# Six products in place of ten for M, with normalized queries regrouped into blocks of 120 features

## The chip, the cores and the metric

One core of one Trainium2 chip. The metric is the device time of one execution in microseconds (us), taken as the median of several runs. Engines are named as the profile names them: PE (TensorE matmul), PEld (its weight loads), DVE (VectorE), ACT (ScalarE), POOL (GpSimd) and SP, whose queue issues most of the DMAs.

## The reference

Two branches are computed from the same x and mixed by a gate. The part that matters here is the linear attention:

```python
B, S, D = 1, 2048, 640;  H = 32;  Dh = 20
pq, pk = phi(q), phi(k)                       # q, k, v = x @ wqkv
kv  = einsum("bhsd,bhse->bhde", pk, v)
num = einsum("bhqd,bhde->bhqe", pq, kv)
den = einsum("bhqd,bhd->bhq", pq, sum_s pk)
a   = (num / den) @ wo
out = g * a + (1 - g) * mlp_branch(x)         # layernorm, w1, shift, w2, layernorm, w3 (F=1728), w4
```

The kernel turns `num @ wo` around: M = blockdiag(kv) @ wo is one 640 x 640 matrix, and a = (pq / den) @ M. The branch with w1 to w4 (called W1 to W4 below) is far more work and shares TensorE with it.

## The kernel before

Every engine has a fixed instruction list. The order of work in it is made while the kernel is built, by a list scheduler that models the engines; each item is placed when its predecessors are done in the model. So any change can reorder the whole list.

M is built from kv, which has blocks of 20 x 20 on the diagonal. Six groups of heads (six heads of 20 features each: 120 rows; the last group has two heads: 40 rows) are multiplied with their rows of wo. M is stored in five tiles of 128 rows, and 120 does not divide 128, so most tiles get rows from two groups: ten products of 640 columns in all. In the code `Lt` holds the masked blocks of kv and `wo_aug` the rows of wo.

```python
PAIRS = []                                   # the ten (group r, tile j) overlaps
for r in range(6):
    f0, f1 = 120 * r, min(120 * r + 120, D)
    j0, j1 = f0 // 128, (f1 - 1) // 128
    for j in range(j0, j1 + 1):
        a0, a1 = max(f0, 128 * j), min(f1, 128 * (j + 1))
        PAIRS.append((r, j, a0, a1))

def m_group(j):
    prs = [(pi, r) for pi, (r, jj, a0, a1) in enumerate(PAIRS) if jj == j]
    b1, b2 = bank(), bank()
    mm_group(ps[:, b1, 0:512], [(Lt[0:nrow(r), pi, :], wo_aug[0:nrow(r), r, 0:512]) for pi, r in prs])
    mm_group(ps[:, b2, 0:128], [(Lt[0:nrow(r), pi, :], wo_aug[0:nrow(r), r, 512:D]) for pi, r in prs])
    activation(M_sb[:, j, 0:512], ps[:, b1, 0:512], ACTF.Copy)
    copy(dve, M_sb[:, j, 512:D], ps[:, b2, 0:128])
# ... cut ...
def qn_scale(t):                             # pq / den, in place, on DVE
    # ... cut: dnr[:, 1, sd, :] = 1 / den
    dve(lambda e: e.tensor_tensor(pq3, pq3, dnr[:, 1, sd, :].unsqueeze(2).to_broadcast([128, H, DH]), ALU.mult), ...)
def qt_tile(t):                              # DMA transpose to pqnT, on the SP queue
    sch.dma("sp", pqnT[:, :, 128 * t:128 * (t + 1)], pq_tok[:, t, :], ..., transpose=True)
def a_tile(t):                               # a = pqn @ M
    # ... cut ...
    mm_group(ps[:, b, 0:512], [(pqnT[:, j, tok], M_sb[:, j, 0:512]) for j in range(KD)])
    mm_group(ps[:, b + 1, 0:128], [(pqnT[:, j, tok], M_sb[:, j, 512:D]) for j in range(KD)])
```

After the last W2 tile, DVE adds its result to x_tok, ACT forms the sum of squares (`junk<-x_tok`), POOL computes the statistics of four tiles (`st`) and normalizes them one by one (`xn<-x_tok,st`), and the SP queue transposes each (`xnT<-xn`). The pqnT transposes stand behind the last of these in the same queue, and the first product with M_sb needs the first pqnT transpose.

## Time and profile before

| | before |
|---|---|
| median of the first 3 runs | 265.46 us (265.42 to 265.71) |
| span of the profiled run | 264.6 us |
| PE busy | 258.2 us, 98% |
| M's ten products on PE | 129.84 to 135.13 us |
| first product with M_sb | 139.58 us |

The profile's page of the kernel before, busy time and instruction counts by engine:

```profile
span 264.6 us, 4264 instructions
## 1 busy us (share of the span) xinstructions
PE 258.2 (98%) x1675; PEld 136.4 (52%) x1707; DVE 145.9 (55%) x242; ACT 107.6 (41%) x216; POOL 91.1 (34%) x148
```

PE is the bound.

PE's timeline of the kernel before, in the stage of M (start us, us until the last end, then line, operation, tiles, shape and count):

```profile
129.84 0.71 PE L606 MATMUL ps<-wo_aug,Lt 120*128 120x512 bf16 x4
130.38 1.24 PE L606 MATMUL ps<-xnT,w_58 128*128 128x512 bf16 x5
131.46 1.25 PE L606 MATMUL ps<-wo_aug,Lt 120*128 120x512 bf16 x8
132.77 1.02 PE L606 MATMUL ps<-xnT,w_58 128*128 128x512 bf16 x4
133.63 1.56 PE L606 MATMUL ps<-wo_aug,Lt 120*128 120x512 bf16 x8
135.13 0.62 PE L1025 MATMUL ps<-xnT,w_58 128*64 128x512 bf16 x4
```

The ten products (each a 512-column and a 128-column matmul) stand in three bursts between W3 groups of five matmuls.

The chain of waits of the kernel before, around the second burst:

```profile
131.66 0.60 ACT h2T L662
132.26 0.50 ACT M_sb L662
132.76 0.01 issue
132.77 2.43 PE ps L606 x12
```

It says that PE waited for ACT to empty a bank at 132.77.

Two lines from POOL's and DVE's timelines of the kernel before become important later, when the first normalization of the last four tiles runs. POOL:

```profile
129.18 0.88 POOL L628 TENSOR_SCALAR xn<-x_tok,st_55 128x640 bf16<-128x640 bf16 x1
```

DVE at that time (the last bracket is idle time ahead of an instruction and what ended it):

```profile
128.42 0.82 DVE L1035 TENSOR_REDUCE dnr<-qprod 128x32 f32<-128x640 f32 x1
130.58 0.29 DVE L671 CAST M_sb<-ps 128x128 bf16<-128x128 f32 x1 [1.35 <-PE ps L606]
```

The normalization took 0.88 us, while DVE stood still for 1.35 us waiting for M's products.

### The profile page before, as it was taken

Reading aid. Unit: us, or ns where it says so; the run is one execution under the profiler, and the core shown is the slowest. Engines: PE = TensorE matmul, PEld = TensorE weight load, DVE = VectorE, ACT = ScalarE, POOL = GpSimd, SP = SyncE. Lnnn points to the kernel's source line nnn. Section 1 sums busy time; section 2 is a strip of 40 time slices with the busy share of each in tenths; the row PEclk is TensorE's granted clock in tenths of the full one; section 3 lists DMA queues with packets and bytes.
Section 4 is the critical chain, followed back from the end, with each engine's and each line's share of the span. In section 5 each row is a group of like instructions: output and inputs, shape, how many; then the busy total and the mean of one; then the engine's idle time right before and its main releaser. Section 6 shows DMA issues by size and latency. Waiting matters only on the chain.

```text
span 264.6 us, 4264 instructions
## 1 busy us (share of the span) xinstructions
PE 258.2 (98%) x1675; PEld 136.4 (52%) x1707; DVE 145.9 (55%) x242; ACT 107.6 (41%) x216; POOL 91.1 (34%) x148
## 2 busy tenths in 40 slices
PE   7999999999999999999999999999999999999996
PEld 3655555555555454554444545554545455545553
DVE  0397877899903797999786886312212121122242
ACT  3486767742365758675661031212211222121000
POOL 4003996849774017487821104001110011021020
DMA  6775898551666895253666731120000200002011
GB/s 203 244 103 147 205 146 149 162 115 24 102 121 104 299 373 82 54 99 60 69 124 124 110 68 25 33 93 0 2 0 0 102 0 0 2 0 99 2 50 50
DMA packets 50595, 24.77 MB, mean 94 GB/s; under 512 B 41996, under 2 KB 49165, under 8 KB 50576
## 3 DMA queue, kind: packets, MB, share of 16 engines
q1 hardware_dynamic: 49328, 21.23, 36.3%
q0 software_dynamic: 1152, 3.28, 5.4%
q8 instruction: 13, 0.21, 0.3%
q14 instruction: 6, 0.05, 0.1%
q10 hardware_dynamic: 96, 0.00, 0.0%
HBM read 12.05 MB, written 2.62 MB: 55 GB/s over the span
## 4 chain that ended last, share of the span: by engine, by line
PE 96%; DMA 1%; issue 1%; ACT 0%; DVE 0%
PE ps L606 60%; PE ps L1103 21%; PE ps L786 8%; PE ps L858 2%; DMA x_tok<-in_A_x_dram 1%; PE ps L1085 1%; PE ps L1025 1%; PE ps L617 1%; PE ps L859 1%; PE ps L944 1%; DVE x_tok L645 0%; PE ps L834 0%; ACT h2T L662 0%; ACT M_sb L662 0%
## 5 line engine op out<-in xcount | busy, mean ns | idle before, releaser
L662 ACT ACTIVATE h2T<-ps 128x512 bf16<-128x512 f32 x52 | 31.0, 597 | 86.5 <-PE ps L606 86.5
L606 PE MATMUL ps<-xnT,w_58 128*128 128x512 bf16 x250 | 59.0, 379 | 0.5
L1103 PE MATMUL ps<-w_84,h2T 128*128 128x128 bf16 (+1 forms) x412 | 58.2, 298 | 0.4 <-issue 0.3
L628 POOL TENSOR_SCALAR abx<-x_tok,stg 128x640 f32<-128x640 bf16 x16 | 13.9, 874 | 107.6 <-DVE x_tok L645 71.0
L1103 PEld LDWEIGHTS ps<-w_84,h2T 128*128 128x128 bf16 x416 | 32.4, 98 | 27.8 <-issue 2.1
L645 DVE SCALAR_TENSOR_TENSOR x_tok<-ps,stg,abx 128x640 bf16<-128x640 f32 (+2 forms) x17 | 14.3, 844 | 50.7 <-PE ps L1103 50.7
L606 PEld LDWEIGHTS ps<-xnT,w_58 128*128 128x128 bf16 x260 | 24.3, 98 | 24.9 <-issue 0.4
L645 DVE SCALAR_TENSOR_TENSOR abx<-ps,stg,abx 128x640 f32<-128x640 f32 x16 | 14.1, 882 | 28.5 <-PE ps L606 25.5
L662 ACT ACTIVATE Er<-ps 128x640 bf16<-128x640 f32 x32 | 22.4, 704 | 12.7 <-PE ps L606 8.5
L662 ACT ACTIVATE hsT<-ps 128x512 bf16<-128x512 f32 (+1 forms) x32 | 18.9, 593 | 14.6 <-PE ps L606 14.3
L661 ACT ACTIVATE junk<-x_tok 128x640 bf16<-128x640 bf16 x32 | 23.6, 736 | 2.0 <-DVE x_tok L643 1.7
L606 PE MATMUL ps<-M_sb,pqnT 128*128 128x128 bf16 (+1 forms) x157 | 23.7, 298 | 0.2
L606 PE MATMUL ps<-w_60,hsT 128*128 128x128 bf16 (+1 forms) x158 | 23.6, 298 | 0.1
L786 PE MATMUL ps<-pk_tok,x_tok 128*128 128x128 bf16 (+1 forms) x156 | 23.3, 297 | 0.2
L606 PE MATMUL ps<-xnT,w_59 128*128 128x512 bf16 x96 | 23.2, 379 | 0.3 <-issue 0.2
L606 PE MATMUL ps<-wkg,xT 128*128 128x131 bf16 (+1 forms) x148 | 22.4, 298 | 0.1
L606 PEld LDWEIGHTS ps<-M_sb,pqnT 128*128 128x128 bf16 x160 | 13.3, 98 | 12.4 <-issue 0.4
L606 PEld LDWEIGHTS ps<-w_60,hsT 128*128 128x128 bf16 x160 | 13.3, 98 | 12.2
L628 POOL TENSOR_SCALAR xn<-x_tok,st_54 128x640 bf16<-128x640 bf16 x16 | 17.4, 1090 | 4.7 <-DMA xnT<-xn 4.6
L606 PE MATMUL ps<-wq,xT 128*128 128x128 bf16 (+1 forms) x118 | 18.2, 298 | 0.1
L628 POOL TENSOR_SCALAR xn<-x_tok,st_55 128x640 bf16<-128x640 bf16 x16 | 16.3, 1028 | 3.6 <-DMA xnT<-xn 3.2
L628 DVE TENSOR_SCALAR Er<-Er 128x640 bf16<-128x640 bf16 x32 | 12.0, 375 | 9.4 <-ACT Er L662 9.2
(74 smaller groups left out, 264.2 us busy)
## 6 DMA issues: line engine op xcount, KB each, us to landing
w_58<-in_B_w_dram SPq DMA_DIRECT2D x1, 2160.0 KB, 8.2
w_84<-in_B_w_dram SPq DMA_DIRECT2D x1, 2080.0 KB, 13.6
x_tok<-in_A_x_dram SPq DMA_DIRECT2D x3, 640.0 KB, 5.5
out_dram<-x_tok SPq DMA_DIRECT2D x3, 640.0 KB, 3.3
wq<-in_A_wqkv_dram SPq DMA_DIRECT2D x5, 160.0 KB, 4.4
wkg<-in_A_wqkv_dram SPq DMA_DIRECT2D x5, 160.0 KB, 4.4
wv<-in_A_wqkv_dram POOLq DMA_DIRECT2D x1, 800.0 KB, 6.3
wo_aug<-in_A_wo_dram POOLq DMA_DIRECT2D x5, 150.0 KB, 5.1
```

The lines of the kernel that those rows point to most:

```text
L606: ins = e.matmul(out_ap, l, r, start=(i == 0), stop=(i == n - 1))
L617: ins = e.transpose(o, s_, ident[:])
L628: return engf(lambda e: e.tensor_scalar(out_ap, in_ap, s1, s2, op0, op1), rd, [out_ap], cost=cost)
L645: return dve(lambda e: e.scalar_tensor_tensor(out_ap, in0, scalar, in1, op0, op1), rd, [out_ap], cost=cost)
L661: return act(lambda e: e.activation(out_ap, in_ap, func, bias=bias, scale=scale, accum_out=accum), rd, wr, cost=cost)
L662: return act(lambda e: e.activation(out_ap, in_ap, func, bias=bias, scale=scale), rd, wr, cost=cost)
L786: ins = e.matmul(o, l, r, start=(t0 + q_ == 0), stop=(t0 + q_ == NT - 1))
L858: e.matmul(ps[:, b, 0:512], l, w[:, k, 0:512], start=(k == 0), stop=(k == KD - 1))
L859: return e.matmul(ps[:, b + 1, 0:n2], l, w[:, k, 512:512 + n2], start=(k == 0), stop=(k == KD - 1))
L944: ins = e.matmul(o, l, r_, start=st_, stop=sp_, skip_group_check=True)
L1025: ins = e.matmul(o, l, r, start=st, stop=sp)
L1103: ins = e.matmul(o, l, r, start=False, stop=(i == KFF - 1))
```

## The change

The features of the normalized queries are regrouped: each block of 128 columns of pq / den now holds the 120 features of one head group, plus 8 of the 40 features of the last two heads. Then a tile of M takes its first 120 rows from one group, and six products are enough. The last two heads' product gives 40 rows, which five small DMAs place in rows 120 to 127 of the five tiles. The scaling multiply writes the new layout and is split in two (600 and 40 elements). To leave its source intact it writes one slot lower, so `pq_tok` has a slot more. M is emptied by ACT alone, and its products are spread out, one after every second W3 group of the first chunk.

```diff
-    pq_tok = pa.alloc("pq_tok", [128, NT, D], BF16)
-    Lt = pa.alloc("Lt", [128, 10, 128], BF16)
+    pq_tok = pa.alloc("pq_tok", [128, NT + 1, D], BF16)
+    Lt = pa.alloc("Lt", [128, 6, 128], BF16)
+    Mt = pa.alloc("Mt", [128, D], BF16)
 ... (the queries are written to slot t + 1; the mask products follow the new layout, six in place of ten)
-    def m_group(j):
-        prs = [...]
-        ... (two banks, products of all pairs of tile j, ACT copies 512 columns, DVE 128)
+    def m_group(r):
+        n = min(R6, D - R6 * r)
+        b = pair()
+        mm_group(ps[:, b, 0:512], [(Lt[0:n, r, :], wo_aug[0:n, r, 0:512])])
+        mm_group(ps[:, b + 1, 0:128], [(Lt[0:n, r, :], wo_aug[0:n, r, 512:D])])
+        src = psf[0:n, 512 * b:512 * b + D]
+        dst = M_sb[0:n, r, :] if r < 5 else Mt[0:n, :]
+        activation(dst, src, ACTF.Copy)
+
+    def m_tail():
+        for j in range(KD):
+            sch.dma("sp", M_sb[R6:128, j, :], Mt[8 * j:8 * j + 8, :], "mt", group_total=KD)
 ...
-    for j in range(KD):
-        IT.add("KVF", ("m", j), 0.57, ..., deps=[(("lt", 0), 2.6), (("lt", 1), 1.0)] if j == 0 else [])
+    for n, r in enumerate((5, 0, 1, 2, 3, 4)):
+        IT.add("KVF", ("m", r), 0.0, ..., deps=[(("lt", 1), 1.0), (("w3", 0, 1 + 2 * n), 0.0)])
+    IT.add("MT", ("mt",), 0.0, m_tail, deps=[(("m", 5), 1.5), (("t1", NT - 1), 0.0)])
 ...
-        dve(... tensor_tensor(pq3, pq3, 1/den broadcast, ALU.mult) ...)          # 640 elements
+        for o, i0, i1, cost in (main, tail):                                     # 600 and 40 elements
+            dve(lambda e, o=o, i0=i0, i1=i1: e.tensor_tensor(o, i0, i1, ALU.mult), ...)
```

More of the change, by code (lines that the diff above doesn't have):

```diff
@@ L842, in q_tile @@
         mm_group(ps[:, b + 1, 0:128], [(xT[:, k, tok], wq[:, k, 512:D]) for k in range(KD)])
-        phi(b, pq_tok[:, t, :])
+        phi(b, pq_tok[:, t + 1, :])
     def stream(order, w, n2, done):
@@ L867, in q_four @@
                  (2, 1), (1, 4), (2, 2), (2, 3), (2, 4), (3, 1), (3, 2), (3, 3), (3, 4)]
-        stream(order, wq, 128, lambda t, b: phi(b, pq_tok[:, t, :]))
+        stream(order, wq, 128, lambda t, b: phi(b, pq_tok[:, t + 1, :]))
     def k_out(t, b):
@@ L917, in _build @@
         IT.add("GT", ("g", i), 1.36, lambda i=i: gt_step(i, NT - 5, NT), deps=[(("g0", NT - 1), 0.0)])
-    PAIRS = []
-    for r in range(6):
-        f0, f1 = 120 * r, min(120 * r + 120, D)
-        j0, j1 = f0 // 128, (f1 - 1) // 128
-        for j in range(j0, j1 + 1):
-            a0, a1 = max(f0, 128 * j), min(f1, 128 * (j + 1))
-            PAIRS.append((r, j, a0, a1))
     kv_bank = {}
@@ L949, in lt_evac @@
         b = kv_bank[h]
-        for pi, (r, j, a0, a1) in enumerate(PAIRS):
-            if (r >= 4) != (h == 1):
-                continue
-            q_ = r - 4 * h
+        for q_, r in enumerate(range(4) if h == 0 else range(4, 6)):
             n = min(R6, D - R6 * r)
-            src = ps[0:n, b, R6 * q_ + a0 - R6 * r:R6 * q_ + a1 - R6 * r]
-            msk = mask[0:n, :, :].rearrange("p b d -> p (b d)")[:, a0 - R6 * r:a1 - R6 * r]
-            tt(dve, Lt[0:n, pi, a0 - 128 * j:a1 - 128 * j], src, msk, ALU.mult)
-        bank_hold.difference_update((b, b + 1))
-    def nrow(r):
-        return min(R6, D - R6 * r)
-    def m_group(j):
-        prs = [(pi, r) for pi, (r, jj, a0, a1) in enumerate(PAIRS) if jj == j]
-        b1, b2 = bank(), bank()
-        mm_group(ps[:, b1, 0:512], [(Lt[0:nrow(r), pi, :], wo_aug[0:nrow(r), r, 0:512]) for pi, r in prs])
-        mm_group(ps[:, b2, 0:128], [(Lt[0:nrow(r), pi, :], wo_aug[0:nrow(r), r, 512:D]) for pi, r in prs])
-        activation(M_sb[:, j, 0:512], ps[:, b1, 0:512], ACTF.Copy)
-        copy(dve, M_sb[:, j, 512:D], ps[:, b2, 0:128])
+            src = ps[0:n, b, R6 * q_:R6 * q_ + n].rearrange("p (h m i) -> p h m i", m=5, i=4)
+            msk = mask[0:n, 0:n // DH, :].rearrange("p h (m i) -> p h m i", i=4)
+            if r < 5:
+                dst = Lt[0:n, r, 0:n].rearrange("p (h m i) -> p h m i", m=5, i=4)
+            else:
+                dst = Lt[0:n, r, 0:n].rearrange("p (m h i) -> p h m i", m=5, i=4)
+            tt(dve, dst, src, msk, ALU.mult)
+        bank_hold.difference_update((b, b + 1))
+    def m_group(r):
[9 more added lines that the diff above has]
+            sch.dma("sp", M_sb[R6:128, j, :], Mt[8 * j:8 * j + 8, :], "mt", group_total=KD)
     def zb_group():
@@ L979, in _build @@
         IT.add("KVF", ("lt", h), 0.0, lambda h=h: lt_evac(h), deps=[(("kvt", h), 0.0)])
-    for j in range(KD):
-        IT.add("KVF", ("m", j), 0.57, lambda j=j: m_group(j), deps=[(("lt", 0), 2.6), (("lt", 1), 1.0)] if j == 0 else [])
+    for n, r in enumerate((5, 0, 1, 2, 3, 4)):
+        IT.add("KVF", ("m", r), 0.0, lambda r=r: m_group(r), deps=[(("lt", 1), 1.0), (("w3", 0, 1 + 2 * n), 0.0)])
+    IT.add("MT", ("mt",), 0.0, m_tail, deps=[(("m", 5), 1.5), (("t1", NT - 1), 0.0)])
     IT.add("ZB", ("zb",), 0.0, zb_group, deps=[(("z", NT - 1), 1.7), (("w2", 0), 0.0)])
@@ L1033, in qn_sum @@
         sd = slot("dnr", 4)
-        tt(dve, qprod[:, :], pq_tok[:, t, :], zb[:, :], ALU.mult)
+        tt(dve, qprod[:, :], pq_tok[:, t + 1, :], zb[:, :], ALU.mult)
         dve(lambda e: e.tensor_reduce(dnr[:, 0, sd, :], qprod[:, :].rearrange("p (h d) -> p h d", d=DH),
@@ L1041, in qn_scale @@
         sd = qn_slot[t]
-        pq3 = pq_tok[:, t, :].rearrange("p (h d) -> p h d", d=DH)
         ts(dve, dnr[:, 0, sd, :], dnr[:, 0, sd, :], EPS_PHI, None, ALU.add, ALU.bypass)
         dve(lambda e: e.reciprocal(dnr[:, 1, sd, :], dnr[:, 0, sd, :]), [dnr[:, 0, sd, :]], [dnr[:, 1, sd, :]], cost=350.0)
-        dve(lambda e: e.tensor_tensor(pq3, pq3, dnr[:, 1, sd, :].unsqueeze(2).to_broadcast([128, H, DH]), ALU.mult),
-            [pq3, dnr[:, 1, sd, :]], [pq3], cost=900.0)
+        blk = pq_tok[:, t, :].rearrange("p (j c) -> p j c", c=128)
+        main = (blk[:, :, 0:R6].rearrange("p j (a d) -> p j a d", d=DH),
+                pq_tok[:, t + 1, 0:5 * R6].rearrange("p (j a d) -> p j a d", a=6, d=DH),
+                dnr[:, 1, sd, 0:30].rearrange("p (j a) -> p j a", a=6).unsqueeze(3).to_broadcast([128, 5, 6, DH]), 850.0)
+        tail = (blk[:, :, R6:128].rearrange("p m (h i) -> p h m i", i=4),
+                pq_tok[:, t + 1, 5 * R6:D].rearrange("p (h m i) -> p h m i", h=2, i=4),
+                dnr[:, 1, sd, 30:32].unsqueeze(2).unsqueeze(3).to_broadcast([128, 2, 5, 4]), 150.0)
+        for o, i0, i1, cost in (main, tail):
+            dve(lambda e, o=o, i0=i0, i1=i1: e.tensor_tensor(o, i0, i1, ALU.mult),
+                [i0, dnr[:, 1, sd, :]], [o], cost=cost)
     def qt_tile(t):
@@ L1188, in _build @@
         c = t // 4
-        deps = [(("qt", t), 3.0), (("w4load",), 0.0), (("m", KD - 1), 1.0)]
+        deps = [(("qt", t), 3.0), (("w4load",), 0.0), (("m", KD - 1), 1.0), (("mt",), 2.5)]
         if t >= 4:
```

## The prediction

> **What bounds the kernel.** TensorE (PE): the page's busy table gives PE 258.2 of 264.6 us (98%), VectorE (DVE) 145.9, ScalarE (ACT) 107.6; the chain that ended last is 96% PE; the clock was 1.00 throughout (windows view). Start-to-start distances in the trace: a 512-column matmul every 216 ns, a 128-column one every 55 ns, with 128 or 120 rows alike. So one 640-column product costs 0.271 us of PE. This agrees with the Trainium skill, "TensorE: Matmul & The Clock Gate", section "Step-by-step: what each phase is for": streaming costs N cycles, the row count does not matter.
>
> **What M costs now.** Ten products (20 matmuls) in three bursts between 129.84 and 135.13 us (timeline) hold the PE for 0.545 + 1.310 + 1.494 = 3.35 us; the ideal is 2.71. The excess:
> - 0.22 us before 132.77, waiting for ACT to empty a bank (the chain passes through ACT h2T and M_sb there).
> - about 0.41 us around the 40-row group: distances of 311 and 320 ns instead of 216, 163 and 155 instead of 55, as 120, 40, 120, 40 rows and a 64-column stage alternate: 0.1 us a switch. The Trainium skill, "TensorEngine Tiling (Array Packing)", "Key Properties", says that changing the tiling mode drains TensorE; the trace agrees.
>
> **What the change does.**
> - PE: 6 products = 1.63 us, one at a time between W3 groups; the 40-row pair stands alone: 2 switches, 0.2 us. Saved: 3.35 - 1.83 = 1.5 us: 1.08 from columns, 0.2 from switches, 0.2 from the bank wait.
> - DVE: five M casts go (1.4 us); ten mask products (2.2 us) become six (estimate 1.7). Each of 16 scaling multiplies (826 ns, 640 elements) becomes 600 elements plus a 40-element tail: estimate 785 + 170, as small ones take 156 to 180; +2 us in all. Net about zero.
> - ACT: six 640-wide evacuations at 0.70 us (as GT's) replace five of 0.594: +1.3 us, off the path.
> - SP queue: 5 small DMAs, 0.43 us of issue each (as weight loads show) = 2.2 us, landing estimated at 2.5. M's first group now runs after W3's second (112 to 113 us), so I expect them near 115 to 118 us, beside a 3.3 us gap in the queue; an xnT transpose may slip 1 to 2 us. The first product that reads M starts at 139.6, so DMAs and M groups (last about 133) have time. The first pqnT transpose is issued at 135.3 and lands about 138; nothing moves it.
>
> **On the path.** PE is the path around this stage and W3 work fills in, so nearly all should reach the end; I take 1.4 us, leaving a little for new stalls.
>
> **Predicted:** 264.0 us, 263.3 to 265.0 in 8 of 10. Faster by over 2%: 0.01; within 2%: 0.975; slower by over 2%: 0.015.
>
> **Signs.** 12 Lt matmuls in six separate pairs, about 112 to 133 us; two long distances at the 40-row pair; no PE wait for ACT M_sb; multiplies of about 780 and 170 ns; PE busy 1.4 us less; M_sb no longer written by DVE; the DMAs landed over 10 us before the first M_sb product.
>
> **What would make it wrong.** The list order of PE work is recomputed: more row-mode switches or bank waits could eat 0.5 us. DVE's tails could delay W2 evacuations and stall PE at 113 to 122 us. The DMAs could block the queue ahead of transposes that W3 or the M products need, costing 1 to 3 us.

## The result

| | before | after |
|---|---|---|
| median, runs of the first comparison (6 each) | 265.65 us (265.42 to 266.42) | 264.90 us (264.68 to 265.59) |
| ratio, 95% interval | | 0.9971 (0.9953 to 0.9989) |
| span of the profiled run | 264.6 us | 263.0 us |

A ratio here is the mean time of one kernel's fast runs over the mean of the other's fast runs of the same rounds, so it is not quite the ratio of the medians. The verdict is "same" at a threshold of 2%: a gain of 0.75 us by the medians, about half of the 1.46 us between 265.46 and the predicted 264.0. The time itself lies inside the predicted range, the size of the gain was wrong.

The page of the changed kernel:

```profile
span 263.0 us, 4293 instructions
## 1 busy us (share of the span) xinstructions
PE 258.2 (98%) x1699; PEld 134.9 (51%) x1699; DVE 146.8 (56%) x249; ACT 108.7 (41%) x217; POOL 93.1 (35%) x148
```

All 1699 matmuls are recorded here, one for each load. The true counts differ by 8, as they should (four products of two matmuls).

The two profiled spans differ by 1.6 us, more than the prediction asked for, and that number misleads. Look at the first product with wkg, long before anything that the change touches. In the timeline of the kernel before:

```profile
12.82 0.38 PE L858 MATMUL ps<-wkg,xT 128*128 128x512 bf16 x1
```

and of the changed kernel:

```profile
11.90 0.38 PE L859 MATMUL ps<-wkg,xT 128*128 128x512 bf16 x1
```

The changed kernel is 0.93 us ahead already (from unrounded starts). In the first microseconds PE's matmuls come at half rate (427 ns for 512 columns), then at 216 ns, and the moment of the switch differs: about 7.6 us in the trace before, about 5.4 us in the trace after. So I read all traces from the first wkg product to the end of the span, and call this the *stretch*: 264.60 - 12.82 = 251.77 us before, 262.97 - 11.90 = 251.07 us after (from unrounded starts). The stretch gained 0.70 us, and that fits the timed runs.

PE's timeline of the changed kernel, the lines that answer to the bursts shown above:

```profile
113.86 0.44 PE L607 MATMUL ps<-wo_aug,Lt 40*128 40x512 bf16 x2
114.23 5.61 PE L607 MATMUL ps<-w,hsT 128*128 128x512 bf16 x40
119.68 3.40 PE L607 MATMUL ps<-xnT,w 128*128 128x512 bf16 x15
122.92 0.44 PE L607 MATMUL ps<-wo_aug,Lt 120*128 120x512 bf16 x2
...
132.65 0.44 PE L607 MATMUL ps<-wo_aug,Lt 120*128 120x512 bf16 x2
133.02 1.27 PE L1022 MATMUL ps<-xnT,w 128*64 128x512 bf16 x10
134.22 5.57 PE L607 MATMUL ps<-xnT,w 128*128 128x512 bf16 x25
140.09 2.18 PE L607 MATMUL ps<-M_sb,pqnT 128*128 128x512 bf16 x13 [0.31 <-DMA pqnT<-pq_tok]
```

In the kernel before, the last of these lines read:

```profile
139.58 2.60 PE L606 MATMUL ps<-M_sb,pqnT 128*128 128x512 bf16 x14
```

The products are spread as planned. The 40-row one comes first, between W2 tiles. The wait in the last line of the changed kernel is new: before the first product with M_sb, PE waits for a pqnT transpose. The page prints 0.31 us, counted from the modelled end of the matmul before; from start to start the distance is 685 ns instead of 216, so 0.47 us are lost.

The chain of waits of the changed kernel, leading to that point:

```profile
132.12 2.65 DMA xnT<-xn
134.77 0.09 issue
134.86 1.18 POOL xn L629
136.04 0.79 POOL abx L629
136.83 0.46 SPq L279
137.29 0.06 issue
137.34 2.71 DMA pqnT<-pq_tok
140.05 0.05 issue
140.09 1.96 PE ps L607 x12
```

The chain has left PE here. It runs through the normalizations of the second layernorm and their transposes, and reaches pqnT in the same queue. Its entries for POOL `abx` and `SPq` cover the time in which the queue issued the last xnT transpose (136.07 to 137.29 us); the first pqnT transpose stands right behind it.

Counted from the first wkg product, the steps of this chain are:

| step, us after the first wkg product | before | after | later by |
|---|---|---|---|
| DVE: last x_tok of W2 starts | 109.42 | 109.97 | 0.55 |
| ACT: its square-sum starts | 112.43 | 113.49 | 1.06 |
| POOL: normalization of tile 12 starts | 116.35 | 118.02 | 1.67 |
| SP: xnT transpose of tile 12 issued | 117.26 | 120.23 | 2.97 |
| SP: first pqnT transpose issued | 122.46 | 125.45 | 2.99 |
| PE: first product with M_sb starts | 126.75 | 128.20 | 1.45 |

The transpose of pqnT was issued 3 us later, and PE's list had put the first M_sb product only about 1 us later (two more W3 groups, ten matmuls or 2.16 us, now stand ahead of it, against 1.08 us of products and 0.1 us of switches saved). Before the change about 1.5 us of slack lay between the landing (2.7 us after the issue) and PE's arrival; 1.5 + 1.0 - 3.0 makes the wait of about 0.5 us.

The largest step, 1.3 us, is the normalization of tile 12 itself. In POOL's timeline of the changed kernel:

```profile
129.92 2.18 POOL L629 TENSOR_SCALAR xn<-x_tok,st 128x640 bf16<-128x640 bf16 x1
```

and in DVE's:

```profile
129.88 0.90 DVE L1049 TENSOR_TENSOR pq_tok<-pq_tok,dnr 128x600 bf16<-128x600 bf16 x2
130.69 0.82 DVE L637 TENSOR_TENSOR qprod<-pq_tok,zb 128x640 f32<-128x640 bf16 x1
```

The same instruction took 0.88 us before. DVE no longer waits for M's products at this point, so its multiply (now two of them) starts 0.04 us ahead of the normalization. The Trainium skill, "SBUF — State Buffer", section "SBUF: two separate sides", describes this: DVE and POOL share a pair of ports under "an exclusive lock, not a bandwidth split", taken by a DVE instruction with two SBUF inputs against a POOL instruction that reads SBUF, and whoever starts first holds it for the whole instruction. All three DVE instructions shown here have two SBUF inputs. The normalization ended at 132.10 us, 0.59 us after the last of them (131.51). The kernel before shows the other order: there POOL was normalizing when DVE's multiply started at 131.38 us, and the multiply took 1.06 us instead of 0.83. That this lock stretched the normalization was a hypothesis at this point; the experiment `dve_waits` tests it.

ACT's queue explains the second step. Its timeline in the changed kernel:

```profile
124.33 0.69 ACT L663 ACTIVATE M_sb<-ps 120x640 bf16<-120x640 f32 x1
124.91 0.60 ACT L663 ACTIVATE h2T<-ps 128x512 bf16<-128x512 f32 x1
125.39 0.74 ACT L662 ACTIVATE junk<-x_tok 128x640 bf16<-128x640 bf16 x1
```

The last square-sum (`junk`) stands behind the emptying of one of M's products. In the kernel before it directly followed the emptying of a W3 bank (`h2T`, 124.78 to 125.37 us):

```profile
125.25 0.73 ACT L661 ACTIVATE junk<-x_tok 128x640 bf16<-128x640 bf16 x1
```

And the five DMAs, in the SP queue of the changed kernel:

```profile
116.09 3.48 SPq L283 DMA_DIRECT2D M_sb<-Mt  x5
119.62 1.22 SPq L279 DMA_TRANSPOSE xnT<-xn  x1
```

They hold the queue for 3.5 us; I had put it at 2.2. The eighth xnT transpose waits behind them.

### The profile page after: what moved, and what is told of

Its sections match the earlier page's. It is cut to its first block, busy times and chain, and to the rows that moved or that the text cites. A ratio compares the mean times of both kernels' runs of the same rounds, so it can differ in the third digit from the quotient of the medians.

```text
span 263.0 us, 4293 instructions
## 1 busy us (share of the span) xinstructions
PE 258.2 (98%) x1699; PEld 134.9 (51%) x1699; DVE 146.8 (56%) x249; ACT 108.7 (41%) x217; POOL 93.1 (35%) x148
## 4 chain that ended last, share of the span: by engine, by line
PE 88%; DMA 3%; POOL 3%; DVE 3%; ACT 1%; issue 1%; SPq 0%; DVEq 0%; POOLq 0%
PE ps L607 53%; PE ps L1107 22%; PE ps L787 8%; PE ps L859 2%; POOL xn L629 1%; DMA x_tok<-in_A_x_dram 1%; PE ps L1089 1%; POOL st L637 1%; DMA pqnT<-pq_tok 1%; DMA xnT<-xn 1%; DVE x_tok L644 1%; PE ps L618 1%; ACT junk L662 1%; PE ps L937 1%; PE ps L860 1%
## 5 line engine op out<-in xcount | busy, mean ns | idle before, releaser
L607 PE MATMUL ps<-xnT,w 128*128 128x512 bf16 x360 | 84.4, 379 | 0.0
L1107 PE MATMUL ps<-w,h2T 128*128 128x512 bf16 (+1 forms) x416 | 58.7, 299 | 0.0
L607 PEld LDWEIGHTS ps<-xnT,w 128*128 128x128 bf16 x360 | 33.4, 98 | 33.8 <-ACT M_sb L663 0.4
L1107 PEld LDWEIGHTS ps<-w,h2T 128*128 128x128 bf16 x416 | 32.4, 98 | 27.8 <-issue 2.1
L629 POOL TENSOR_SCALAR xn<-x_tok,st 128x640 bf16<-128x640 bf16 x32 | 35.5, 1115 | 8.8 <-DMA xnT<-xn 8.3
L607 PE MATMUL ps<-M_sb,pqnT 128*128 128x512 bf16 (+1 forms) x160 | 23.7, 299 | 0.3 <-DMA pqnT<-pq_tok 0.3
L607 PE MATMUL ps<-w,hsT 128*128 128x512 bf16 (+1 forms) x160 | 23.9, 299 | 0.0
L787 PE MATMUL ps<-pk_tok,x_tok 128*128 128x512 bf16 (+1 forms) x160 | 23.9, 299 | 0.0
L607 PE MATMUL ps<-wkg,xT 128*128 128x512 bf16 (+1 forms) x150 | 22.6, 299 | 0.0
L607 PE MATMUL ps<-wq,xT 128*128 128x512 bf16 (+1 forms) x120 | 18.3, 299 | 0.0
```

The costliest lines, as they stand in the source:

```text
L607: ins = e.matmul(out_ap, l, r, start=(i == 0), stop=(i == n - 1))
L629: return engf(lambda e: e.tensor_scalar(out_ap, in_ap, s1, s2, op0, op1), rd, [out_ap], cost=cost)
L787: ins = e.matmul(o, l, r, start=(t0 + q_ == 0), stop=(t0 + q_ == NT - 1))
L1107: ins = e.matmul(o, l, r, start=False, stop=(i == KFF - 1))
```

## The experiments

**Theories.** Mine: the M stage on PE gained about 1.2 us; about 0.45 us was given back in the wait for the first pqnT transpose, because its chain got 3 us later (inserted work on PE and ACT, and the loss of port time on POOL); the 0.93 us at the start is chance; and the bank wait of 0.22 us that I had counted as a gain never existed. The rivals are A: the early start comes with the change (a smaller memset of Lt); B: the wait is a fluke; C: the stage is bound by the transposes, so taking one wait away only moves it; D: POOL was slowed by something else than DVE, or the DMA queue delayed the chain.

**How the kernels were made.** A reordering by the list scheduler would mix causes. So most experiments replay the order of items that the scheduler had found (the change's own, or that of before), written out as a list, with only the named items moved. The short diffs below leave out the list and this replay routine. The number that I read in each trace is the stretch, which repeats within 0.05 us (251.77 and 251.78 before, 251.07 and 251.02 after). The timed runs scatter by about 1 us; the start is in them, and in the traces it alone moves by 1.2 us. So the timed runs show that most of these kernels lie below the kernel before (not before_padded), but not the differences of some tenths between them: those rest on the stretch, with one trace for each experiment.

### after_again and before_again: second traces, unedited

> The changed kernel itself, unedited, for a second trace and more times. My theory: the profiled pair differed by 1.6 us, of which 0.93 us was already there 13 us after the start (before M is touched) and belongs to the moment at which TensorE leaves its half rate, which I hold to be chance; the M stage gave 1.2 us, and 0.47 us was given back in one PE wait for the first pqnT transpose at 139.4 us. Then the times should again be about 0.75 us below before (ratio 0.997), the trace should again show the wait of about 0.47 us ahead of the first M_sb product, and the start of the first wkg product may fall anywhere between 11.9 and 12.9 us. Rival A: the early start comes with the change (its memset of Lt is smaller); then the first wkg product starts at 11.9 us again, here and in every kernel built from the changed one, and at 12.8 in every kernel built from before. Rival B: the 0.47 us wait was a fluke of that run; then it is not there now and the ratio is nearer 0.995.

> The kernel before, for a second trace. My theory: the distance of 276 ns between the last 128-column product of M's third group and the next W3 matmul at 132.5 us was no wait for a bank but one missing matmul record (55 + 216 + 5 ns), and so were two distances of 375 ns after the 64-row products. In this trace M's second burst (four products) should then take 1.08 us up to the next W3 matmul, without a gap, or show the same 276 only if the record is lost again. If the wait was real, a gap near 0.22 us is there again with five W3 matmuls in every group. The first wkg product starts anywhere from 11.9 to 12.9 us if chance sets the start; rival A expects 12.8.

The changed kernel: ratio 0.9978 (0.9955 to 1.0), 265.5 against 266.15 us; stretch 251.02 us; the wait is there again with 0.43 us. Its first wkg product starts at 12.31 us. Before: stretch 251.78 us, first wkg product at 12.64 us. Rival B falls.

PE's timeline of this second trace of the kernel before, at the place of the supposed bank wait:

```profile
131.28 1.25 PE L606 MATMUL ps<-wo_aug,Lt 120*128 120x512 bf16 x8
132.37 1.24 PE L606 MATMUL ps<-xnT,w 128*128 128x512 bf16 x5
133.45 1.56 PE L606 MATMUL ps<-wo_aug,Lt 120*128 120x512 bf16 x8
```

Eight matmuls in 1.09 us, four times 0.271, then a W3 group of five. There is no gap. In the first trace the group had four, and the distance of 276 ns was the one lost record (55 + 216 + 5). This trace has 1707 matmuls for 1707 loads. The same holds for two distances of 375 ns later in the first trace: none here. The chain of waits had filled the hole with ACT instructions that happened to end there.

### late_a0: one W3 group ahead of the first product with M_sb

```diff
 # order of items
+ ('w3', 1, 5)
  ('a', 0) ... ('a', 1) ('a', 2) ... ('w4', 1) ...
- ('w3', 1, 5)
```

> The changed kernel with its own order of work replayed from a list, and one W3 group (the sixth of the second chunk, 1.08 us of PE) moved ahead of the first product with M_sb. Only PE's order differs. My theory (the wait of 0.47 us for the first pqnT transpose is a real loss, and PE had other work at hand): the wait before the first M_sb product falls to 0, no new one takes its place, and the time falls by 0.47 us against the changed kernel, ratio to before about 0.9954. Rival C (the whole stage behind it is bound by the chain of transposes, so PE only waits elsewhere): the wait reappears before the next M_sb products or later, and the time stays as it is in the changed kernel, ratio 0.997.

Only PE's list differs. PE's timeline of this kernel:

```profile
139.28 2.54 PE L655 MATMUL ps<-xnT,w 128*128 128x512 bf16 x11
141.65 1.52 PE L655 MATMUL ps<-M_sb,pqnT 128*128 128x512 bf16 x10
```

No wait is left in front of the M_sb products, and none appears later. The stretch is 250.59 us, 0.45 less than the mean of the two traces of the change (251.05). Ratio 0.9952 (0.9929 to 0.9974). Rival C falls: the wait was a real loss, and one group of other work would have filled it. The first pqnT transpose was issued just as late as in the change (125.43 us after the first wkg product, 125.45 and 125.41 there), so it is the position in PE's list that decides, not the chain alone. The first wkg product started at 12.84 us, although this kernel has the change's smaller memset.

### six_of_ten: the columns alone

```diff
-        prs = [(pi, r) for pi, (r, jj, a0, a1) in enumerate(PAIRS) if jj == j]
+        prs = [(pi, r) for pi, (r, jj, a0, a1) in enumerate(PAIRS) if jj == j][0 if j == KD - 1 else 1:]
```

> The kernel before, its order of work replayed, with four of the ten M products left out (wrong result on purpose: the first product of the first four groups of M). Nothing else changes, so this measures what PE columns alone are worth: 4 x 0.271 = 1.08 us. The switches between 120 and 40 rows stay. My theory: the time falls by 1.08 us (ratio 0.9959), as PE before the change reached the first M_sb product about 1.5 us after the pqnT transpose had landed, so 0.4 us of that slack is left. Rival C (the stage is bound by the transposes): under 0.5 us. If the bank wait of 0.22 us that I saw in the first trace was real and is caused by the bursts of M products, it could go as well, and 1.3 us fall away.

The result is wrong on purpose (relative error 0.035). The stretch is 250.67 us, 1.10 less than before, as expected (1.08). Ratio 0.9961 (0.9937 to 0.9985). The first wkg product started at 11.71 us, the earliest of all, in a kernel with the larger memset of before.

### dve_waits: DVE's multiply after the normalizations

```diff
-    ts(pool, xn[:, sx, :], x_tok[:, t, :], ...)
+    n_ev[(which, t)] = ts(pool, xn[:, sx, :], x_tok[:, t, :], ...)
 ...
-            dve(lambda e, ...: e.tensor_tensor(o, i0, i1, ALU.mult), [i0, dnr[:, 1, sd, :]], [o], cost=cost)
+            sch.op("dve", lambda e, ...: e.tensor_tensor(o, i0, i1, ALU.mult), [i0, dnr[:, 1, sd, :]], [o],
+                   deps=[n_ev[(2, 14)]] if t == 8 else [], cost=cost)
```

> The changed kernel, its order replayed, with one wait added on VectorE: the scaling multiply of tile 8 waits for the third normalization of the last chunk (tile 14) on GpSimd. In both traces of the changed kernel that multiply starts 20 to 40 ns before the first of these normalizations (tile 12), which then takes 2.18 us instead of 0.88; in the kernel before VectorE stood waiting for M's products at that moment and the normalization took 0.88. My theory: the two engines exclude each other, and that 1.3 us is the largest part of the 2.96 us by which the chain to the first pqnT transpose got later. Then the normalization of tile 12 takes about 0.9 us, the last xnT transposes and the first pqnT transpose come 1.3 us earlier (first pqnT issue at about 124.1 us after the first wkg product, from 125.4), the PE wait of 0.43 to 0.47 us is gone, and the stretch from the first wkg product to the end falls from 251.05 to 250.6 us. Rival D (GpSimd was slowed by something else, or the chain is held by the transposes' queue): the normalization stays above 1.5 us, or the pqnT transpose does not move and the wait stays.

POOL's timeline of this kernel, the normalization of tile 12:

```profile
130.97 0.89 POOL L677 TENSOR_SCALAR xn<-x_tok,st 128x640 bf16<-128x640 bf16 x1
```

and DVE's, the multiply that now waits:

```profile
133.69 0.78 DVE L1098 TENSOR_TENSOR pq_tok<-pq_tok,dnr 128x600 bf16<-128x600 bf16 x1 [2.79 <-POOL xn L677]
```

With DVE idle the normalization takes 0.89 us instead of 2.18. Its transpose is issued 1.24 us earlier (118.96 us after the first wkg product, from 120.20), the first pqnT transpose 1.0 us earlier (124.42), the PE wait is gone, and the stretch is 250.59 us. A part of the gain was lost again: the normalization of tile 15 now met the postponed multiply (1.46 us). The ratio of the timed runs, 0.9971 (0.9952 to 0.9991), does not show the 0.45 us; its interval is 1.04 us wide, more than twice that. Rival D falls as far as the length of the normalization goes: it is DVE's activity that stretches it. That the shared ports are the reason is the page's reading.

### m0_later: M's first product after the last square-sum

```diff
 # order of items
- ('m', 0)          # ahead of ('sq', 15)
  ('sq', 15) ... ('s2', 3)
+ ('m', 0)
```

> The changed kernel, its order replayed, with the product of M's first 120 rows moved three W3 groups later, so that ScalarE empties it after the last square-sum and not before it. My theory: the last square-sum, 113.49 us after the first wkg product, comes 0.5 us earlier (113.0, the rest of its delay being the inserted 40-row pair), the statistics and the first normalization follow at about 117.5, which is before VectorE's multiply at 117.97, so that the normalization takes 0.9 us; the pqnT transpose then comes 1.5 us or more earlier, and the PE wait is gone: 250.6 us for the stretch. Rival D expects at most 0.5 us at the transpose, which would still remove the wait of 0.43 us; what tells them apart is the length of the normalization, 0.9 against 2.2 us.

The square-sum came 0.58 us earlier (112.91), the normalization of tile 12 started at 117.21 and took 0.88 us, the first pqnT transpose was issued 1.8 us earlier (123.62), the wait is gone, and the stretch is 250.59 us. Ratio 0.9962 (0.9943 to 0.9982). So the emptying of M's product on ACT, 0.5 us of delay by itself, was what brought POOL into collision with DVE. The collision did not vanish, it moved: the normalization of tile 14 took 2.08 us here, where less hung on it.

### m5_later: the 40-row product after the W2 tiles

```diff
 # order of items
- ('m', 5)  ('w2', 12)  ('mt',)  ('w2', 13)  ('t2', 7) ... ('w2', 15) ... ('t2', 8)
+ ('w2', 12)  ('w2', 13)  ('t2', 7) ... ('w2', 15)  ('m', 5) ... ('t2', 8)  ('mt',)
```

> The changed kernel, its order replayed, with the 40-row product moved from between the W2 tiles to after the last of them, and its five DMAs two transposes later. It measures what that insertion and the DMAs ahead of the transposes cost the chain. My theory: the last x_tok comes 0.46 to 0.55 us earlier (109.45 after the first wkg product); square-sum, VectorE's multiply and the normalization all move by about the same, so the collision of normalization and multiply remains (2.2 us), and the pqnT transpose comes only about 0.5 us earlier; the PE wait of 0.43 us just vanishes or stays under 0.1 us: 250.6 us for the stretch. If the queue of DMAs had held the transposes, the transpose would come over 1.5 us earlier with the normalization still at 2.2 us.

This one missed. The last x_tok did come 0.43 us earlier (109.53), but the square-sum did not move (113.50): it stands on ACT behind the emptying of M's next product, and PE reached that one at the same time as before. POOL's statistics then took longer than in the change (0.57 to 0.83 us for steps of 0.20), the normalization of tile 12 started at 119.06 but took 0.88 us, that of tile 14 took 2.08. The first pqnT transpose came at 125.47, the PE wait was 0.49 us, the stretch 251.09 us (ratio 0.997, 0.9953 to 0.9987). So the pair inserted between the W2 tiles is not what delays the chain, as long as ACT's order holds it later; and the collision of POOL and DVE is not one unlucky instruction but wanders over what POOL does there.

### one_multiply: the scaling in one operation

```diff
-        for o, i0, i1, cost in (main, tail): dve(... tensor_tensor(o, i0, i1, ALU.mult) ...)
+        o  = pq_tok[:, t, :].rearrange("p (h d) -> p h d", d=DH)       # the old layout
+        i0 = pq_tok[:, t + 1, :].rearrange("p (h d) -> p h d", d=DH)
+        dve(lambda e: e.tensor_tensor(o, i0, dnr[...] broadcast, ALU.mult), ..., cost=900.0)
```

> The changed kernel, its order replayed, with each tile's scaling multiply done by one operation on 640 elements again, without the layout that M now needs (wrong result on purpose). It measures what the split costs. From the trace the two parts take 783 and 195 ns against 826 for one, with starts 0.70 us apart, so one operation should free VectorE by about 0.11 to 0.15 us a tile. My theory: over three tiles since the last x_tok the multiply of tile 8 starts about 0.3 us earlier and VectorE is done with it and the following product about 0.45 us earlier; GpSimd's normalization of tile 12 then takes 1.7 to 1.9 us instead of 2.18, the first pqnT transpose comes 0.3 to 0.5 us earlier, and the PE wait falls to under 0.15 us (stretch 250.6 to 250.75 us). If the split has no part in the delay, the normalization stays at 2.2 us and the wait at 0.43.

The parts of the change take 783 and 195 ns, one operation 824 to 826. The first pqnT transpose came only 0.16 us earlier (125.25), less than the 0.3 to 0.5 expected; the normalization of tile 12 started later (118.68, its statistics were slowed) and took 1.34 us. The wait fell from 0.43 to 0.27 us, the stretch to 250.88 us; ratio 0.9964 (0.9938 to 0.9991). So the split has a part of about 0.17 us. Its output is wrong, which doesn't matter for the time. The comparison with the reference does not test the placing of features. That the change's layout is right I checked only by following the indices.

### one_dma: one of the five DMAs

```diff
-        for j in range(KD):
-            sch.dma("sp", M_sb[R6:128, j, :], Mt[8 * j:8 * j + 8, :], "mt", group_total=KD)
+        for j in range(1):
+            sch.dma("sp", M_sb[R6:128, j, :], Mt[8 * j:8 * j + 8, :], "mt", group_total=1)
 ...
+    memset(pool, M_sb[:], 0.0)
```

> The changed kernel, its order replayed, with one of the five DMAs that place M's last rows (the other rows stay zero from a memset: wrong result on purpose). It measures what the DMAs cost the transposes behind them. In the trace the five take the queue from 116.09 to 119.58 us (3.5 us, 0.63 to 0.77 each) and hold the eighth xnT transpose. My theory: that transpose comes about 2.7 us earlier, but the last chunk's chain does not start with it, so the first pqnT transpose moves by less than 0.3 us, the normalization of tile 12 still collides and the PE wait stays between 0.2 and 0.5 us (stretch about 251.0). If the DMAs were what delayed the chain (one of the ways in which the prediction said it could fail), the transpose comes over 1 us earlier and the wait is gone.

The eighth xnT transpose came 2.65 us earlier (105.05 us after the first wkg product, from 107.70), and the first pqnT transpose only 0.1 us (125.32). The normalization of tile 12 still collided, but differently: it started at 118.64 and took 1.44 us. The wait was 0.34 us, the stretch 250.94 us, ratio 0.9973 (0.9953 to 0.9994). The DMAs hold the queue longer than I had thought and still cost the chain about 0.1 us. Its output is wrong, which doesn't matter for the time.

### before_padded and late_padded: no 40-row product

```diff
+    memset(pool, wo_aug[:, 5, :], 0.0)              # both
-    def nrow(r):
-        return min(R6, D - R6 * r)
+    def nrow(r):                                    # before_padded
+        return R6
-        mm_group(ps[:, b, 0:512], [(Lt[0:n, r, :], wo_aug[0:n, r, 0:512])])
+        mm_group(ps[:, b, 0:512], [(Lt[0:R6, r, :], wo_aug[0:R6, r, 0:512])])   # late_padded, on top of late_a0
```

> The kernel before, its order replayed, with the 40-row product of M padded with zeros to 120 rows, nothing else. It measures what the row-mode switches were worth in the kernel before. My theory: of the four excesses of 95, 103, 109 and 100 ns the first three go, and the fourth stays, as the next stage has 64 columns; 0.31 us less, and the stretch from the first wkg product to the end falls from 251.78 to 251.47 us. M's second burst again shows no bank wait if all records are there.

> The version with one W3 group moved ahead of the first M_sb product, and with the last product of M padded with zeros from 40 to 120 rows (a memset at the start), so that TensorE does not switch its row mode for it. My theory: the two long distances (96 and 93 ns of excess) at that pair go, 0.19 us; the stretch from the first wkg product to the end falls from 250.59 to 250.40 us, the result stays correct, and the time is about 0.995 of before or a little less. A rival, that the excess belongs to a product standing alone between other work, expects 250.59 again.

Before, padded: stretch 251.47 us, 0.31 less. Three of the four excesses at the 40-row product are gone, and the fourth is paid by the stage of 64 columns that follows. In the timed runs (0.9994, 0.997 to 1.0017) this is not visible. One record was lost again at M's second burst, which again left a hole of 276 ns and a W3 group of four.

On late_a0: PE's timeline at the padded product,

```profile
114.76 0.44 PE L655 MATMUL ps<-wo_aug,Lt 120*128 120x512 bf16 x2
115.25 1.02 PE L655 MATMUL ps<-w,hsT 128*128 128x512 bf16 x4
```

has one W2 matmul record missing (115.25 - 0.216 = 115.03, which is 0.27 us after the product began). In late_a0 the product with 40 rows stands 0.37 us ahead of the next work:

```profile
114.81 0.44 PE L655 MATMUL ps<-wo_aug,Lt 40*128 40x512 bf16 x2
115.18 1.04 PE L655 MATMUL ps<-w,hsT 128*128 128x512 bf16 x4
```

The stretch is 250.39 us, 0.21 less than late_a0; ratio to before 0.9954 (0.9936 to 0.9971), result correct. The Trainium skill, "TensorEngine Tiling (Array Packing)", section "Key Properties", says that a change of the tiling mode drains TensorE. The traces agree that 40 rows between 120 or 128 cost something, 0.09 to 0.11 us for each change, and zeros up to 120 rows remove it. That the mode is the cause is the page's reading; the runs show the cost and its removal.

### All traces side by side

| kernel | first wkg product | stretch | PE wait before M_sb |
|---|---|---|---|
| before (two traces) | 12.82, 12.64 us | 251.77, 251.78 us | 0 |
| before_padded | 12.26 | 251.47 | 0 |
| six_of_ten | 11.71 | 250.67 | 0 |
| after (two traces) | 11.90, 12.31 | 251.07, 251.02 | 0.47, 0.43 |
| m5_later | 12.36 | 251.09 | 0.49 |
| one_dma | 12.56 | 250.94 | 0.34 |
| one_multiply | 11.95 | 250.88 | 0.27 |
| dve_waits | 12.93 | 250.59 | 0 |
| m0_later | 12.12 | 250.59 | 0 |
| late_a0 | 12.84 | 250.59 | 0 |
| late_padded | 12.89 | 250.39 | 0 |

Three different ways of removing the wait end at the same 250.59 us. The starts lie between 11.71 and 12.93 us without regard to the kernel they belong to, so rival A falls. The Trainium skill, "TensorE: Matmul & The Clock Gate", section "What's actually happening", gives a reason: the clock is released by an activity window that runs freely, so that the moment of the switch varies by 500 ns either way. The traces agree that it varies, but it varies more: the spacing of the matmuls halves at about 4.9 us in six_of_ten and at about 7.9 us in dve_waits. The first wkg product moves by 1.2 us between the extremes. That the window is the cause is the page's reading.

## Why the prediction was right or wrong

The time (264.9 us) was inside the range and the direction was right, but the gain was 0.73 us in the stretch (251.774 - 251.048, means of two traces each) where the prediction counted 1.5 and took 1.4. Term by term:

| term of the sum | predicted | measured |
|---|---|---|
| four products fewer on PE | 1.08 us | 1.10 (six_of_ten) |
| fewer row-mode switches | 0.2 | 0.10: 0.31 (before_padded) less 0.21 (late_padded against late_a0) |
| "0.2 from the bank wait" | 0.2 | 0: a lost matmul record |
| new waits | -0.1 | -0.45 (late_a0 against the change) |
| sum | 1.4 | 0.75; the stretch itself gives 0.73 |

- **Right:** PE was the bound and a product was worth 0.271 us. The spread of the products, the two long distances at the 40-row pair, the shapes and times of the DVE multiplies (783 and 195 ns for the predicted 785 and 170), and the DMAs issued 20 us before the first M_sb product (116.1 to 119.6 and 140.1 us) came as written.
- **Wrong, first step:** "0.22 us before 132.77, waiting for ACT to empty a bank". The second trace shows no gap there. I trusted a chain of waits over a count: the W3 group had four matmuls instead of five, and the page had 32 fewer matmuls than loads.
- **Wrong, second step, and the larger one:** "The first pqnT transpose is issued at 135.3 and lands about 138; nothing moves it." It moved by 3 us against the rest of the kernel, used up the 1.5 us of slack and left PE waiting 0.43 to 0.47 us. The steps are an ACT evacuation ahead of the last square-sum (shown by m0_later), and POOL's normalization held up by DVE, which before the change happened to stand idle waiting for M (dve_waits shows the hold-up, the first trace the idle DVE). The split multiply and the DMAs added about 0.17 and 0.1 us (one_multiply, one_dma).
- **Sized wrong, without much effect:** the fourth switch at the 40-row group before the change belongs to the stage of 64 columns that follows and stays (147 ns instead of 55 in the changed kernel), so 0.1 us of the predicted 0.2 was not saved; the DMAs take 3.5 us of the queue, not 2.2.
- **The listed risks:** the prediction named DMAs that block the queue and DVE tails that delay W2. The DMAs did hold the queue, for a small part of the delay; the tails moved the last W2 addition by about 0.06 us (one_multiply), and PE did not stall at 113 to 122 us. Neither was the main cause. It did not name POOL, though the normalizations run on it.
- The sign "PE busy 1.4 us less" cannot be read from the first pair: 258.2 us in both, but 32 matmul records are missing in the trace of the kernel before, and the half-rate time at the start counts as busy. The complete traces show it: from the first wkg product on, PE is busy 249.19 us in before_again and 248.17 and 248.18 us in the two traces of the change, 1.0 us less. Of that the page's 0.31 us of idle time at the new wait is lost again, and 0.7 us are left.
- **Open:** how the 3 us divide exactly. The collisions of DVE and POOL moved to other instructions with every shift, so the contributions do not add up. Nor is it shown for each slowed POOL statistics step which DVE instruction held it.

The version with the shortest stretch is late_padded: 250.39 us, 0.66 below the change and 1.39 below before (0.9954 of before in the timed runs, 0.9936 to 0.9971). Against the change the timed runs do not separate it: its interval overlaps with the change's (0.9953 to 0.9989).

## What to carry to other kernels

When one engine bounds a kernel and its list is fixed, work saved on it lets it arrive earlier at its next dependency: measure the slack at that point before counting the saving, and check what the change adds to every engine in that dependency's chain. A wait that is removed on one engine (here DVE's wait for M) starts that engine's next work earlier, and on engines that share a port it may hit a chain that had run alone by luck. Before trusting a gap of one instruction's length in a trace, count the instructions around it, and measure from a mark after the start, where the runs differ by chance.

## What the Trainium skill lacked or had wrong

- "SBUF — State Buffer" has the exclusive lock between DVE and POOL, and the runs agree with it. It lacks a size for a case like this: a 128x640 normalization on POOL went from 0.88 to 2.18 us beside three DVE instructions in a row (783, 195 and 819 ns) and ended 0.59 us after the last of them, so it seems that POOL did not get its turn between them.
- "TensorEngine Tiling (Array Packing)" gives no cost for a change of mode. Measured: 0.09 to 0.11 us for each, and padding a 40-row product to 120 rows with zeros removed 0.21 us (two changes) and 0.31 us (three).
- "Perfetto Trace Analysis" does not say that a trace can lack matmul records and that the comparison of matmul and load counts reveals it: 1675 for 1707 in one trace of the kernel before, 1707 for 1707 in the other.
- "TensorE: Matmul & The Clock Gate" puts the variation of the switch to the full clock at 500 ns either way (its 6, 11 or 14 slow matmuls for one and the same kernel are a wider spread). Here it fell between about 4.9 us (six_of_ten) and 7.9 us (dve_waits), and moved the first wkg product by 1.2 us. That is more than the effect under study (0.73 us), so the traces had to be compared from a mark behind the start.
